# Talking-heads attention and two gated layers: another f64 conversion, and the last hand-over put into the plan

## The chip, the cores and the metric

The kernel runs on one core of a Trainium2 chip. The metric is the time of one execution on the device in microseconds (us), lower is better. The engines named here are PE (TensorE: matrix products; PEld is its weight load), DVE (VectorE: elementwise and reductions), ACT (ScalarE: activation functions and copies), POOL (GpSimd, which here only issues transfers) and SP (SyncE, which also issues transfers). A transfer that an engine's queue issues is written as SPq, ACTq or POOLq.

## What is computed

Attention in which the twelve heads are mixed before and after the softmax, then two layers of gated products. The weights of the two layers arrive as float64, so they have to be made float32 on the chip.

```python
scores = scale * np.matmul(q, k.transpose(0, 1, 3, 2))          # 4 batches, 12 heads, 448 x 448, 64 deep
scores = np.einsum('bhij,hg->bgij', scores, w_pre)
attn = exp(scores - max) / (sum + 1e-9)
attn = np.einsum('bhij,hg->bgij', attn, w_post)
x = np.matmul(attn, v)                                           # as 1792 rows of 768
x = ((x @ w1) * (x @ w2)) @ w3 @ w_out                           # 768 -> 1024 -> 768
out = np.maximum(np.maximum(x @ m1, x @ m2), x @ m3) @ m_out     # 768 wide
```

## The kernel before

**Attention** goes through 92 steps, 23 of 20 query rows for each of the four batches. Scores are computed by `unit` (PE line 345), evicted from PSUM by ACT or DVE (lines 360 and 362), stored in DRAM (`sdram`) and read back in another layout (`x`) by `regroup`. A step mixes heads (408), takes maxima and exponentials (412, 415), multiplies by the second mixing (446) and copies out (275). Every six steps `attend` multiplies by v (480). For batches 1 to 3 its result goes through the tile `xs` into DRAM (`xdram`).

**The dense work.** Before anything else the product of w3 and w_out is formed once (`fuse_parts`, line 606, result `w34`). Then batch 0 goes through the layers while batches 1 and 2 are in attention, and batch 1 while batch 3 is (`dense_parts`, line 687). Each product of float32 quality is three passes of a faster format, so every operand is split: ACT copies it to the high part (`hi`), DVE subtracts to get the low part (`lo`). A weight slab of 128 x 768 sits in one of three slab tiles (`whi`, `wlo`); `prepare` loads the slab two jobs ahead. Each of the last layer's six slabs ("o") takes 18 matmuls. Batches 2 and 3 come last and together (`last_two`), by a scheme of seven products instead of eight (`seven`, matmuls of line 219), on operands that are sums and differences of their rows: named t1, t2, t3, t4 and 22, three chunks (k = 0, 1, 2) of 128 x 448 each, and 11 and 21, which are rows of batch 2.

**Conversion of the weights** (`convert`, lines 504 to 531). A tile of float64 words is loaded by POOL's queue into `wraw` (three buffers; for w_out the tile `early`, in six places). Of each word, word(1) is its upper half and word(0) its lower. Then one ACT operation (522) and four of DVE (523, 525, 527, 529) build the float32 bits in `wc` (for w_out in the tile `v`). There are 40 tiles of 768 columns, 16 of 512 (w3) and 16 of 384 (w_out). After that ACT and DVE split it (655 and 656, 536 and 538, 571 and 572). The buffer is free for the next load when the last DVE operation has read it.

**What sets the order.** Up to the end of attention every instruction is an entry of `plan`, with an engine or a choice of two, an assumed duration, a due time and what it reads and writes. `Plan.order` runs through these with its own model and writes each engine's instructions down in the order found; each engine then executes its list strictly in order. So an instruction that waits holds up all behind it on its engine. What follows the plan is written by hand: `rest_of_one` multiplies batch 1 by the six "o" slabs (loads 236, splits 237 and 238, matmuls 219, evictions 1086, stores by ACT's queue 1087), and `attention_operands` is woven in between, one piece for every pair of chunks multiplied: it loads t3, 22, t1 and t4 from `xdram` by ACT's queue (764) and calls `layer_operands`, which subtracts (791) and splits (749, 750). These tiles lie in a pool `last` that is opened when the pool `pa` of the attention has been closed, so their loads wait until the last users of `pa` are done. The last of those are the two stores of `xs` into `xdram` after the last `attend`.

Of the kernel before, what the change touches and what calls it, by code (L numbers as in the profile page):

```python
# [8 lines left out]
F32 = mybir.dt.float32  # L9
# [28 lines left out]
F64_MIN = 2.0 ** -15  # L38
F64_MAX = 122880.0

# [135 lines left out]
def attention_talking_heads_moe_kernel(  # L176
# [327 lines left out]
    def convert(key, src, w, after=(), early=None):  # L504
# [10 lines left out]

        def word(x):
            return to().bitcast(U32).rearrange("p (x two) -> p x two", two=2)[:, :, x]
# [119 lines left out]
    KEPT = len(DENSE) - KX  # L637
# [114 lines left out]
    def attention_operands(X):  # L752

        last = tail["pool"]
        rows = tail["x"] = {}
        for n, name in enumerate(("11", "21")):
            rows[name] = [[t[:, n * QK + k] for k in range(QK)] for t in X[APART]]
        f = {}
        for name, b, x in (("t3", 1, 0), ("22", 1, 1), ("t1", 0, 0), ("t4", 0, 1), ("t2", 0, 2)):
            hi, lo = (last.tile([P, QK, S], F32R, tag=name + y, name=name) for y in ("hi", "lo"))  # L760
            rows[name] = [[t[:, k] for k in range(QK)] for t in (hi, lo)]
            if x < 2:
                f[name] = lo.bitcast(F32)
                nc.scalar.dma_start(f[name], xdram[APART + b][x * QK:(x + 1) * QK].rearrange("x p i -> p x i"))
        yield
        for k in range(QK):
            v = {"11": f["t1"][:, k], "21": f["t4"][:, k], "12": f["t3"][:, k], "22": f["22"][:, k]}
            yield from layer_operands(rows, k, v, ("11", "21"))
# [72 lines left out]
    def weight_groups(name, i, n):  # L841

        yield split_group(kept[name, i], 2 * HW)
# [249 lines left out]
    for _ in rest_of_one():  # L1093
        step()
# [49 lines left out]
```

## Time and profile before

| what | before |
|---|---|
| time, median of 3 runs (lowest to highest) | 1164.87 us (1164.27 to 1166.12) |
| the profiled execution's own time | 1165.8 us |
| its span from first to last instruction | 1164.0 us |
| PE busy | 1104.3 us (95%) |
| DVE busy | 839.9 us (72%) |
| ACT busy | 542.8 us (47%) |
| chain that ended last, by engine | PE 81%, DMA 10%, DVE 4%, ACT 2% |
| granted PE clock, mean of the span | 0.975 of full speed |

Busy times come from one profiled execution. "Busy" of PE counts overlapping matmuls of modelled length, so the step from the start of one matmul to the start of the next is the better measure of PE's pace. A row of a timeline gives start and length in us, engine, line, operation, output and inputs, shape, and in brackets how long the engine had been idle and what ended that. A trailing x2 means two in a row in one row.

### The profile page before, as it was taken

To read this page: it belongs to the slowest core of one execution; us is meant where nothing else is said; L and a number is where in the kernel's file an instruction comes from. 1 tells how busy PE (TensorE), PEld (TensorE's weight loads), DVE (VectorE), ACT (ScalarE), POOL (GpSimd) and SP (SyncE) were. 2 spreads that over 40 slices of the span, in tenths; PEclk is the share of its full clock that TensorE was granted. 3 is DMA by queue.
4 is the path that set the end of the run, shared out by engine and by line. 5 is a ranking of instruction groups with operands and counts; after the bars stand their busy time and mean duration, and the time that the engine had idled before them with its cause. 6 is when DMAs were issued, how large, how long until landed. Compare 5 with 4: busy or idle time off the path is not lost.

```text
span 1164.0 us, 29307 instructions
## 1 busy us (share of the span) xinstructions
PE 1104.3 (95%) x12348; PEld 892.4 (77%) x12348; DVE 839.9 (72%) x1452; ACT 542.8 (47%) x1034; POOL 74.5 (6%) x141
## 2 busy tenths in 40 slices
PE   3689999999999999999999999998899999999998
PEld 0256768777878778787876778877788899988987
DVE  3788777788965888987666678772877754587874
ACT  3455554565565656555444454442533334332331
POOL 3010000000000000000111101110000000000000
PEclk8579999999999999999999999999899999999999
DMA  8889879869995797989999898965433321233343
GB/s 253 244 278 307 264 224 325 257 221 323 300 321 155 254 308 255 346 280 303 303 287 305 286 308 281 309 200 194 153 99 109 107 85 50 75 109 109 102 117 122
DMA packets 118318, 259.82 MB, mean 223 GB/s; under 512 B 23446, under 2 KB 72106, under 8 KB 118186
## 3 DMA queue, kind: packets, MB, share of 16 engines
q1 hardware_dynamic: 97994, 172.75, 46.7%
q0 software_dynamic: 15584, 77.62, 20.4%
q10 hardware_dynamic: 4608, 7.57, 1.8%
q8 instruction: 97, 1.59, 0.6%
q14 instruction: 35, 0.29, 0.1%
HBM read 175.13 MB, written 82.77 MB: 222 GB/s over the span
## 4 chain that ended last, share of the span: by engine, by line
PE 81%; DMA 10%; DVE 4%; ACT 2%; issue 1%; POOL 0%; SPq 0%; ACTq 0%; DVEq 0%; POOLq 0%
PE w L687 26%; PE w L219 9%; PE p L446 7%; PE p L219 6%; PE p L480 6%; PE m L219 6%; PE s L219 6%; PE m L408 6%; PE s L345 5%; PE w L606 5%; DMA sdram<-s 2%; DMA wraw<-in_wa 1%; DMA sdram<-a 1%; DMA early<-in_w_out 1%; DMA t<-xdram 1%
## 5 line engine op out<-in xcount | busy, mean ns | idle before, releaser
L446 PEld LDWEIGHTS p<-kwr,e 60*64 60x64 f32 x5760 | 103.6, 137 | 43.3 <-issue 29.1
L415 ACT ACTIVATE e<-m,nmax 128x448 f32<-128x448 f32 (+1 forms) x184 | 115.3, 635 | 39.0 <-DVE nmax L412 38.9
L412 DVE TENSOR_REDUCE nmax<-m 128x2 f32<-128x896 f32 (+1 forms) x92 | 100.1, 1088 | 43.2 <-PE m L408 42.6
L446 PE MATMUL p<-kwr,e 60*64 60x60 f32 x5760 | 106.1, 221 | 3.7 <-DVE kwr L422 1.7
L275 ACT COPY a<-p 128x480 f32<-128x480 f32 (+1 forms) x109 | 59.9, 574 | 96.9 <-PE p L446 91.6
L408 PE MATMUL m<-x,kp 60*64 60x448 f32 x720 | 91.9, 564 | 7.7 <-ACT e L415 4.9
L345 PE MATMUL s<-kall,q 64*64 64x448 f32 x640 | 82.7, 587 | 15.5 <-DMA q<-in_qT 10.2
L687 PE MATMUL w<-yhi,whi 128*128 128x448 f32 x216 | 82.8, 383 | 0.1
L687 PE MATMUL w<-yhi,wlo 128*128 128x448 f32 x216 | 79.2, 367 | 0.8 <-DVE wlo L663 0.8
L687 PE MATMUL w<-ylo,whi 128*128 128x448 f32 x216 | 79.0, 366 | 0.0
L480 PEld LDWEIGHTS p<-a,v 128*64 128x64 f32 x1536 | 73.7, 137 | 6.8 <-issue 3.9
L480 PE MATMUL p<-a,v 128*64 128x120 f32 (+1 forms) x1536 | 78.0, 261 | 0.0
L687 PE MATMUL w<-xhi,whi 128*128 128x448 f32 x192 | 74.5, 388 | 0.7 <-DVE t L275 0.5
L687 PE MATMUL w<-xhi,wlo 128*128 128x448 f32 x192 | 70.5, 367 | 1.8 <-DVE wlo L663 1.8
L687 PE MATMUL w<-xlo,whi 128*128 128x448 f32 x192 | 70.2, 365 | 0.0
L749 ACT CAST whi<-wlo 128x768 fp32r<-128x768 f32 x40 | 33.4, 835 | 76.6 <-DMA wlo<-sums_m 20.8
L360 ACT ACTIVATE s<-s 128x896 f32<-128x896 f32 x52 | 47.7, 917 | 38.3 <-PE s L345 28.7
L275 DVE COPY a<-p 128x480 f32<-128x480 f32 x71 | 46.0, 654 | 23.2 <-ACT a L275 18.2
L219 PE MATMUL p<-t,vhi 128*128 128x448 f32 x204 | 61.7, 373 | 0.0
L663 DVE TENSOR_TENSOR wlo<-wlo,whi 128x768 fp32r<-128x768 f32 (+1 forms) x46 | 47.0, 1022 | 19.8 <-ACT whi L662 19.6
L522 ACT ACTIVATE wc<-wraw 128x768 f32<-128x768 f32 (+1 forms) x56 | 47.4, 848 | 28.7 <-DMA wraw<-in_w3T 8.5
L749 ACT CAST vhi<-vlo 128x768 fp32r<-128x768 f32 (+1 forms) x40 | 26.9, 674 | 68.9 <-DMA vlo<-sums_m 22.1
(226 smaller groups left out, 2610.2 us busy)
## 6 DMA issues: line engine op xcount, KB each, us to landing
x<-sdram SPq DMA_DIRECT2D x176, 210.0 KB
sdram<-s SPq DMA_DIRECT2D x66, 448.0 KB
wraw<-in_wm POOLq DMA_DIRECT2D x18, 768.0 KB, 6.6
wlo<-kept_m SPq DMA_DIRECT2D x27, 384.0 KB
wlo<-kept_w SPq DMA_DIRECT2D x18, 512.0 KB
wraw<-in_w3T POOLq DMA_DIRECT2D x16, 512.0 KB, 7.3
kept_m<-wc SPq DMA_DIRECT2D x18, 384.0 KB
wc<-kept_m POOLq DMA_DIRECT2D x18, 384.0 KB, 7.1
```

Of the source, the lines that this page charges most:

```text
L219: nc.tensor.matmul(out, w, r, start=(k == 0), stop=(k == 3 * n_k - 1))
L275: (nc.scalar.copy if e == "ACT" else ENG[e].tensor_copy)(out, src)
L345: nc.tensor.matmul(pt[HB * c:HB * c + HB, o, :S], qs[slot][sl, pr, i:i + HB], kall[sl, pr], start=True, stop=True)
L360: nc.scalar.activation(out, pt[:, :, :S], AF.Copy, scale=D ** -0.5)
L408: nc.tensor.matmul(pm[HB * c:HB * c + HB, u, :S], kp[sl], x[sl, c], start=True, stop=True)
L412: plan("DVE", 1.1, key + 0.01, lambda _: nc.vector.tensor_reduce(out=nmax[:r], in_=pm[:r, :, :S], axis=AX.X, op=ALU.max, negate=True), m_b ...
L415: plan("ACT", 0.85, key + 0.02, lambda _, u=u: nc.scalar.activation(e_[:r, u], pm[:r, u, :S], AF.Exp, bias=nmax[:r, u:u + 1], scale=1.0, a ...
L446: nc.tensor.matmul(pt[HB * side:HB * side + HB, c, t, :, u * GB:u * GB + m], e_[sl, u, j:j + HB], kwr[sl, u, :, :m], start=True, stop=True,)
L480: nc.tensor.matmul(pt[o * D:(o + 1) * D, x, pr % 3, :], vt[:, jc, h * D:(h + 1) * D], a[:, jc, h, :], start=(jc == 0), stop=(jc == JC - 1),)
L606: nc.tensor.matmul(pw[b][:, :FW], w, r, start=(k == 0 and i == 0), stop=(k == KH - 1 and i == 2))
L687: nc.tensor.matmul(pw[w][:, :S], u, r, start=(k == 0 and i == 0), stop=(k == nk - 1 and i == 2))
L749: nc.scalar.copy(hi, t)
```

## The change

Two things change, apart from the names in code that follows from them.

`convert` builds the float32 bits in another way. DVE clamps word(1), read as float32 with its sign, to plus or minus 122880 (one operation, from the strided `wraw` to `wc`). ACT then applies a parametric relu that scales by 2^-112 and gives negative values a slope of -2^32, so that the sign ends up as a bit of the exponent. A second ACT operation, which needs nothing of these, copies word(0) in place as an integer scaled by 7.49 * 2^-32, which leaves its top three bits. One DVE operation shifts `wc` left by three and ors these bits in. ACT has two operations for one, DVE two for four. ACT still loads its table of functions once, as before.

The hand-over at the end of the plan is now in the plan. Batch 1's "o" jobs are the last jobs of `dense_parts` (so `rest_of_one` is gone, and their stores go by SP's queue). `attention_operands` is replaced by `tail_parts`, a fifth stream of the plan: closing `pa` and opening `last`, the four loads by SP's queue, the differences and splits, and the first two weight groups of `last_two`, each with a due time. The lists `weight_groups` and `whole_slab` give functions instead of tiles, so that the first two groups can be skipped where they were made already.

```diff
-        plan("ACT", 0.88 * f, key, lambda _: nc.scalar.activation(t, word(1).bitcast(F32), AF.Abs), raw, wc)
         plan("DVE", 0.14 + 0.43 * f, key, lambda _: nc.vector.tensor_scalar(
-            t, t, F64_MIN, F64_MAX, op0=ALU.max, op1=ALU.min), (), wc)
-        plan("DVE", 0.14 + 0.43 * f, key, lambda _: nc.vector.tensor_scalar(
-            ti, ti, 5, 2, op0=ALU.logical_shift_left, op1=ALU.logical_shift_right), (), wc)
+            t, word(1).bitcast(F32), -F64_MAX, F64_MAX, op0=ALU.max, op1=ALU.min), raw, wc)
+        plan("ACT", 0.08 + 0.76 * f, key, lambda _: nc.scalar.activation(
+            t, t, AF.Prelu, scale=EXPONENT, alpha=SIGN), (), wc)
+        plan("ACT", 0.08 + 0.84 * f, key, lambda _: nc.scalar.activation(word(0), word(0), AF.Copy, scale=TOP), raw, low)
         plan("DVE", 0.16 + 0.8 * f, key, lambda _: nc.vector.scalar_tensor_tensor(
-            ti, word(0), 29, ti, op0=ALU.logical_shift_right, op1=ALU.bitwise_or), raw, wc)
-        plan("DVE", 0.16 + 0.8 * f, key, lambda _: nc.vector.scalar_tensor_tensor(
-            ti, word(1), 0xC0000000, ti, op0=ALU.bitwise_and, op1=ALU.bitwise_or), raw, wc)
+            ti, ti, 3, word(0), op0=ALU.logical_shift_left, op1=ALU.bitwise_or), raw + low, wc)
...
+    def tail_parts(pool_users, at_):
...
+        def move(_):
+            stages.close()
+            last = tail["pool"] = ctx.enter_context(tc.tile_pool(name="last", bufs=1))
...
+        n = plan("SP", 0.0, at_(0), move, (), [("moved",)])
+        plan.ops[n][3].update(pool_users)
...
+        for name, b, x in names[:4]:
+            dma("SP", at_(1), lambda name=name: tiles[name][1].bitcast(F32),
+                xdram[APART + b][x * QK:(x + 1) * QK].rearrange("x p i -> p x i"), 688e3,
+                [("moved",)] + [("xd", APART + b, c, x) for c in range(NCH)], [("l", name, k) for k in range(QK)])
...
+        def difference(k, x, y, reads):
+            n = turn("r", 3)
+            plan("DVE", 0.63, at_(3 + k), lambda _: nc.vector.tensor_sub(spares[n], x(), y()), reads, [("r", n)])
...
+        def split(k, name, value):
+            src, reads = value
+            plan("ACT", 0.57, at_(3 + k), lambda _: nc.scalar.copy(tiles[name][0][:, k], src()), reads, [("h", name, k)])
+            plan("DVE", 0.64, at_(3 + k), lambda _: nc.vector.tensor_sub(
...
-        yield from dense_parts(1, DENSE[:KEPT], second_at)
+
+    def second_stream():
+
+        yield TURN + 0.01
+        yield from dense_parts(1, DENSE, second_at)
+
+    def tail_stream():
+
+        yield second_at(126.5)
+        yield from tail_parts(pool_users, lambda x: LAST + 2.2 + 0.8 * x)
...
-    behind.append(attention_operands(X))
-    for _ in rest_of_one():
-        step()
-    flush()
+    for g in tail["made"]:
+        next(tail["groups"])
+        made.append(g)
     for _ in last_two():
         step()
```

SP's list at the hand-over, from the last slabs of the layer before to the first weight groups. `kept_o` are the "o" slabs, `xdram_82` is batch 3 and `xdram_81` batch 2, `t` and `22` the operands. Before:

```order
L270 DMA wlo<-kept_m_5_118 128x768
L236 DMA wlo<-kept_o_119 128x768
L236 DMA wlo<-kept_o_120 128x768
L270 DMA xdram_82<-xs 128x3x88 x2
L236 DMA wlo<-kept_o_121 128x768
L837 DMA vlo<-sums_a_125 128x768
L236 DMA wlo<-kept_o_122 128x768
L837 DMA vlo<-kept_a_93 128x384
```

After:

```order
L272 DMA wlo<-kept_m_5_118 128x768
L272 DMA wlo<-kept_o_119 128x768
L272 DMA xdram_82<-xs 128x3x88 x2
L272 DMA wlo<-kept_o_120 128x768
L272 DMA t_8795<-xdram_82 128x3x448
L272 DMA 22_8797<-xdram_82 128x3x448
L272 DMA t_8799<-xdram_81 128x3x448
L272 DMA wlo<-kept_o_121 128x768
L272 DMA t_8801<-xdram_81 128x3x448
L272 DMA wlo<-kept_o_122 128x768
```

The four operand loads moved from ACT's queue into SP's, the second "o" slab now stands behind the stores of `xs`, and the third and fourth stand among the operand loads.

DVE's list at the same place: maxima of the layer before (717, now 718), low parts of "o" slabs (238, now 664), differences (791, now 788) and their low parts (750, now 794). Before:

```order
L238 TENSOR_TENSOR wlo<-wlo,whi 128x768 x2
L717 TENSOR_TENSOR t<-w,t 128x448
L704 TENSOR_TENSOR hlo<-t,hhi 128x448
L791 TENSOR_TENSOR t_8909<-t_8890,t_8896 128x448
L791 TENSOR_TENSOR t_8917<-22_8893,t_8909 128x448
L238 TENSOR_TENSOR wlo<-wlo,whi 128x768
```

After:

```order
L664 TENSOR_TENSOR wlo<-wlo,whi 128x768
L718 TENSOR_TENSOR t<-w,t 128x448
L705 TENSOR_TENSOR hlo<-t,hhi 128x448
L277 COPY t<-w 128x448
L788 TENSOR_TENSOR r<-t_8795,t_8799 128x448
L788 TENSOR_TENSOR r<-22_8797,r 128x448
L794 TENSOR_TENSOR t_8799<-r,t_8798 128x448
L788 TENSOR_TENSOR r<-22_8797,t_8795 128x448
L664 TENSOR_TENSOR wlo<-wlo,whi 128x768
```

The third slab's low part stands behind a difference of t3 and t1 in both lists; before it two more operations stand there now, and the eviction of the first "o" product has come to DVE.

DVE's list where the tiles of w_out are converted (`early` is the float64 tile, `v` the result, `hlo` its low part). Before:

```order
L525 TENSOR_SCALAR v<-v 128x384
L572 TENSOR_TENSOR hlo<-v,hhi 128x384
L527 SCALAR_TENSOR_TENSOR v<-early,v 128x384
L525 TENSOR_SCALAR v<-v 128x384
L529 SCALAR_TENSOR_TENSOR v<-early,v 128x384
L527 SCALAR_TENSOR_TENSOR v<-early,v 128x384
L523 TENSOR_SCALAR v<-v 128x384
```

After:

```order
L526 TENSOR_SCALAR v<-early 128x384 x2
L574 TENSOR_TENSOR hlo<-v,hhi 128x384
L531 SCALAR_TENSOR_TENSOR v<-v,early 128x384
L526 TENSOR_SCALAR v<-early 128x384
L531 SCALAR_TENSOR_TENSOR v<-v,early 128x384
L574 TENSOR_TENSOR hlo<-v,hhi 128x384 x2
L531 SCALAR_TENSOR_TENSOR v<-v,early 128x384
L526 TENSOR_SCALAR v<-early 128x384
```

Five DVE operations for a tile have become three, and ACT's relu (528) lies between the first and the second of them. In the whole program 17 evictions of scores moved from ACT to DVE (360, 362: 52 and 26 before, 35 and 43 after).

## Rows read from the trace of the kernel before

**Rows 1.** Windows by stage: busy us of each engine, granted clock, DMA share, GB/s.

```profile
45.00:90.00 45.00, 36.10 (x218) 23.25 (x218) 38.07 (x96) 25.50 (x50) 7.93 (x14) 0.75 0.83 267
...
225.00:570.00 345.00, 343.20 (x4902) 271.90 (x4898) 273.90 (x454) 198.31 (x383) 22.25 (x41) 1.00 0.86 281
...
797.00:837.00 40.00, 31.12 (x217) 28.20 (x216) 22.05 (x35) 16.85 (x31) 0.00 (x0) 0.87 0.57 189
```

**Rows 2.** Timeline of PE across the hand-over: start us, length us, operation.

```profile
801.67 0.47 PE L687 MATMUL w<-yhi,whi 128*128 128x448 f32 x1
...
802.99 0.36 PE L219 MATMUL w<-hhi,whi 128*128 128x448 f32 x1
...
810.08 0.37 PE L219 MATMUL w<-hhi,wlo 128*128 128x448 f32 x1
819.33 0.74 PE L219 MATMUL w<-hhi,whi 128*128 128x448 f32 x1 [8.88 <-ACT o L1086]
...
825.04 0.37 PE L219 MATMUL w<-hhi,whi 128*128 128x448 f32 x1
...
836.59 0.37 PE L219 MATMUL m<-xhi,whi 128*128 128x448 f32 x1
```

**Rows 3.** Timeline of ACT across the hand-over.

```profile
801.78 0.66 ACT L275 COPY xs<-p 128x264 f32<-128x264 f32 x2 [1.06 <-PE p L480]
...
804.78 0.41 ACTq L764 DMA_DIRECT2D t<-xdram  x1
...
807.50 0.84 ACT L237 CAST whi<-wlo 128x768 fp32r<-128x768 f32 x1 [3.08 <-PE w L219]
```

**Rows 4.** Timeline of DVE across the hand-over.

```profile
817.62 0.62 DVE L791 TENSOR_TENSOR t<-t,t 128x448 f32<-128x448 f32 x1 [12.55 <-DMA t<-xdram]
...
818.82 0.95 DVE L238 TENSOR_TENSOR wlo<-wlo,whi 128x768 fp32r<-128x768 f32 x1
```

**Rows 5.** Timeline of SP's queue across the hand-over.

```profile
802.19 0.90 SPq L270 DMA_DIRECT2D xdram<-xs  x2
803.21 0.45 SPq L236 DMA_DIRECT2D wlo<-kept_o  x1
```

**Rows 6.** Window of the wait at the hand-over, columns as in rows 1.

```profile
810.00:815.00 5.00, 0.45 (x3) 0.07 (x1) 0.00 (x0) 0.00 (x0) 0.00 (x0) 0.97 1.05 394
```

**Rows 7.** Groups by line and shape: count, busy us, mean ns, idle before.

```profile
L522 ACT ACTIVATE wc<-wraw 128x768 f32<-128x768 f32 x40 | 36.7, 918 | 20.2 <-DVE wlo L656 6.0 <-DMA wraw<-in_wa 5.4 <-DMA kept_b<-wc 3.0
L655 ACT CAST whi<-wc 128x768 fp32r<-128x768 f32 x40 | 33.4, 836 | 12.8 <-DVE wc L529 7.1 <-PE w L687 5.6
L523 DVE TENSOR_SCALAR wc<-wc 128x768 f32<-128x768 f32 x40 | 22.2, 555 | 13.8 <-ACT wc L522 13.5
L527 DVE SCALAR_TENSOR_TENSOR wc<-wraw,wc 128x768 uint32<-128x768 uint32 x40 | 38.2, 954 | 0.6
```

**Rows 8.** Windows while the tiles of w_out are converted, columns as in rows 1.

```profile
50.00:55.00 5.00, 3.14 (x10) 2.31 (x11) 5.00 (x14) 3.03 (x7) 1.61 (x3) 0.84 0.73 215
...
65.00:70.00 5.00, 4.09 (x23) 2.56 (x23) 3.67 (x10) 3.95 (x8) 0.68 (x2) 1.00 0.99 386
...
80.00:85.00 5.00, 3.96 (x18) 2.33 (x15) 4.55 (x10) 3.22 (x5) 0.00 (x0) 0.50 0.33 129
```

**Rows 9.** Timeline of DVE while the tiles of w_out are converted.

```profile
55.17 0.55 DVE L529 SCALAR_TENSOR_TENSOR v<-early,v 128x384 uint32<-128x384 uint32 x1
...
57.12 0.55 DVE L529 SCALAR_TENSOR_TENSOR v<-early,v 128x384 uint32<-128x384 uint32 x1
```

**Rows 10.** Timeline of ACT in the same stretch.

```profile
52.55 0.99 ACT L522 ACTIVATE v<-early 128x384 f32<-128x384 f32 x2
...
76.64 0.56 ACT L522 ACTIVATE v<-early 128x384 f32<-128x384 f32 x1 [1.03 <-DMA early<-in_w_out]
```

**Rows 11.** PE's waits from 90 to 797 us: total us, times, longest.

```profile
PE w L687 <- DVE wlo L663: 2.6, 4, 1.1
PE m L408 <- ACT e L415: 2.3, 2, 1.2
```

More of the change, by code (lines that the diff above doesn't have):

```diff
@@ L37 @@
 RB = 6
-F64_MIN = 2.0 ** -15
 F64_MAX = 122880.0
+EXPONENT = 2.0 ** -112
+SIGN = -2.0 ** 32
+TOP = 7.49 * 2.0 ** -32
 def blocks_of(p):
@@ L514, in convert @@
             raw = [(f"X{'hl'[z]}", x)]
+        low = [("low", raw[0])]
         def word(x):
@@ L636, in attention_talking_heads_moe_kernel @@
     DENSE += [(KX, (f"m{x}", m)) for m in range(KX) for x in range(3)] + [(KX, ("o", m)) for m in range(KX)]
-    KEPT = len(DENSE) - KX
     def dense_parts(b, jobs, at_):
@@ L841, in weight_groups @@
     def weight_groups(name, i, n):
-        yield split_group(kept[name, i], 2 * HW)
-        yield split_group(sums[name, i][:, :2 * HW], 2 * HW)
-        yield split_group(sums[name, i][:, 2 * HW:], 2 * HW)
-        yield split_group(kept[name, i + n][:, HW:], HW)
+        yield lambda: split_group(kept[name, i], 2 * HW)
+        yield lambda: split_group(sums[name, i][:, :2 * HW], 2 * HW)
+        yield lambda: split_group(sums[name, i][:, 2 * HW:], 2 * HW)
+        yield lambda: split_group(kept[name, i + n][:, HW:], HW)
     def whole_slab(m):
-        yield [t.rearrange("p k f -> p (k f)") for t in slab(KH, ("w34", m))]
+        yield lambda: [t.rearrange("p k f -> p (k f)") for t in slab(KH, ("w34", m))]
     def all_groups():
@@ L870, in look_ahead @@
                 break
-            made.append(g)
+            made.append(g())
     def group():
@@ L917, in last_two @@
     def last_two():
-        x = tail["x"]
+        x = {name: [[t[:, k] for k in range(QK)] for t in pair] for name, pair in tail["tiles"].items()}
+        for n, name in enumerate(("11", "21")):
+            x[name] = [[t[:, n * QK + k] for k in range(QK)] for t in rows("X")]
         last = tail["pool"]
@@ L1060, in summing @@
         yield from sum_parts(sums_at)
-    streams = [attention_parts(), dense_stream(), summing()]
-    heads = [(-20.0 + x, x) for x in range(3)]
+    streams = [attention_parts(), dense_stream(), summing(), second_stream(), tail_stream()]
+    heads = [(-20.0 + x, x) for x in range(5)]
     heapq.heapify(heads)
+    pool_users = []
     while heads:
         _, x = heapq.heappop(heads)
+        n = len(plan.ops)
         key = next(streams[x], None)
+        if x < 3:
+            pool_users += range(n, len(plan.ops))
         if key is not None:
@@ L1072, in attention_talking_heads_moe_kernel @@
         plan.emit()
-    X = {APART: rows("X")}
-    def rest_of_one():
-        ready = [slab(KX, ("o", m)) for m in range(2)]
-        for m in range(KX):
-            hi, lo = ready.pop(0)
-            pt = bank()[:, :S]
-            zh, zl = rows("H")
-            yield from products(pt, [(hi[:, k], lo[:, k], zh[:, k], zl[:, k]) for k in range(KX)], KX)
-            if m + 2 < KX:
-                ready.append(slab(KX, ("o", m + 2)))
-            o = scratch("o")
-            nc.scalar.copy(o, pt)
-            nc.scalar.dma_start(outT[m * P:(m + 1) * P, S:2 * S], o)
-    stages.close()
-    tail["pool"] = ctx.enter_context(tc.tile_pool(name="last", bufs=1))
     tail["groups"] = all_groups()
-    behind.append(attention_operands(X))
-    for _ in rest_of_one():
-        step()
-    flush()
+    for g in tail["made"]:
+        next(tail["groups"])
+        made.append(g)
     for _ in last_two():
```

49 lines of the change are left out of this document (34 added, 15 removed).

## The prediction

> **What bounds the kernel now.** I read the windows by stage first, then PE's timeline where a window is not full, then the lists of the engines that PE waited for. From 225 to 570 us PE is busy 343.20 of 345 us at full clock, while DVE is busy 273.90 and ACT 198.31 [rows 1]: there PE sets the time, and a cheaper conversion is worth only what it takes away of PE's own waits. Over the whole stretch from 90 to 797 us these are 8.6 us in eight groups, the two largest 2.6 and 2.3 [rows 11]. So the time is to be looked for in two stages. From 45 to 90 us PE is busy 36.10 of 45 at a mean clock of 0.75, and from 797 to 837 us 31.12 of 40 at 0.87 [rows 1].
>
> At the hand-over PE steps from 802.99 to 810.08 in 35 matmuls, 0.203 us each, stops for 8.88, and then takes 5.71 us for the 15 matmuls up to 825.04, where 15 at 0.203 would be 3.04 [rows 2]. The granted clock in the 15 is the lower of the two levels (0.5 of full); it fell during the idle time. From the end of attention's last product (801.67) to the first matmul of the seven products (836.59) are 34.92 us for 6 + 108 matmuls, which at 0.203 need 23.1. **The hand-over costs 11.8 us.** Its cause stands on DVE: the low part of the third "o" slab (818.82) waits in line behind a difference that waits 12.55 us for the operand loads [rows 4], issued by ACT at 804.78 [rows 3], after the stores of `xs` at 802.19 [rows 5]. The core's transfers run at 394 GB/s meanwhile [rows 6].
>
> From 45 to 80 us the sixteen tiles of w_out are converted. DVE is busy all 5.00 us of a window while the transfers move 215 GB/s; fifteen us later ACT and DVE wait for tiles that arrive, at 386 GB/s [rows 8, 10]. A tile takes DVE 1.95 us (57.12 less 55.17) [rows 9]. PE's products need these tiles in order.
>
> **The hand-over, part by part.** I count from A, the end of the last attention product (801.67 before). The order puts 24 matmuls of the layer before and of the first slab behind it (six before), then the rest of the 108.
> - The `xs` stores are issued at about A+0.5, the second "o" slab right behind them, at A+1.5 (the third slab's place before: 803.21 [rows 5]); before it went ahead of them. A load issued there was in place by A+5.8, when ACT's copy of it began [rows 3]. Copy 0.84, low part 0.95: A+7.6. PE gets to it after 36 matmuls, at A+7.3, and has to wait for the maximum on DVE that frees the PSUM bank, queued behind that low part: A+8.0. **A wait of 0.7.**
> - The operand loads follow at A+3.1 (804.78 before). t3, 22 and t1 are 2.06 MB, 5.3 us at 394 GB/s [rows 6]; with 1.8 ahead of the first byte and some 1.5 behind the last (estimates: the wait before was 12.8 from the issue at 804.78 to 817.62, with 3.5 to 4.1 MB moving, 9 to 10 us at that rate) they are there at A+11.5 to A+12. Here they have the queue nearly to themselves, since the third slab's load must wait for PE to free its tile at A+7.3 and stands behind them. The fourth load, t4, is held up by this one and lands at about A+14.5.
> - PE finishes the first slab at A+11.7 and the second at A+12.9 (12 + 6 + 6 matmuls after A+8.0). ACT then evicts the second (0.5), copies t1 (0.57) and only then the third slab (0.84): A+14.8. DVE does four operations of 0.55 to 0.62 and that slab's low part: A+16.1. PE waits 1.9, does two matmuls, and waits 0.9 more. **Together 2.8.** After that the lists are ahead of PE: the fourth slab's low part ends at A+19.3 and PE arrives there at A+19.35.
> - The last k of the operands is ready at about A+35: DVE has some 24 us of operations from A+11.7 on, and PE needs the last t3 at about A+37. That holds by two us.
>
> So 3.5 us of waits stay of 11.8, in pieces of at most 2 us, and the clock stays up: **-8.3 us.** Bounds: if the loads are there sooner all goes (-11.8); if they are there as late as before, or the clock falls in the waits as well, 4 to 5 more stay (-3.5). What hides the differences and splits now is the 22 us of "o" products, and the cover is thin: DVE is full from A+12 to A+35.
>
> **The conversion, part by part.** A tile of 768 columns costs ACT 0.918 and DVE 2 x 0.555 + 2 x 0.954 = 3.02 before [rows 7]. After, DVE does one operation like 527 (0.954) and a clamp. The clamp reads every second word of `wraw`, which 523 does not: 0.555 if that costs nothing, 0.954 if it runs as slowly as 527, which does read so; I take 0.555, the row of the same operation. ACT does the relu, in rows between 0.836 (a copy of dense words) and 0.918 (strided), and the integer copy, 0.918, with a strided output that no row shows; up to 1.0. DVE falls by 1.1 to 1.5 us a tile, ACT rises by 0.84 to 1.0. In tiles of 768 there are 58.7 (40 + 16 x 2/3 + 16 x 1/2), so DVE loses 65 to 88 us of work and ACT gains 49 to 59, less 17 evictions moved to DVE. From 225 to 570 neither fills up: ACT would come to about 220 of 345 and DVE to about 235 [rows 1]. So there it lies beside PE.
>
> The Trainium skill ("VectorE: DVE Perf Modes", What auto-detection actually checks) says that an operation of one source, with source and destination in SBUF and their outermost dimensions even, is done two elements at a time, and asks no dense words of it for 32-bit data. By that the clamp costs 0.555; at 0.954 ACT and DVE would be level below and the stage would gain some 2 us less. No row before shows a strided clamp.
>
> From 45 to 80 us it is on the path. A tile of 384 takes DVE there 1.95; without two operations of 0.27 and 0.47 step it is 1.2 to 1.4. ACT's three operations step by 0.42 to 0.45 (two in 0.99 less the overlap [rows 10]): 1.3 a tile, 21 us for sixteen. Added to this are about five evictions of scores at 0.9 and an exponential pair that now stands here: 28 us from about 46, so the last tile at 74, where DVE took until 78 before. ACT takes DVE's place as the limit, and the transfers are a second limit close to it (386 GB/s near the end [rows 8]). **-3 us, between 0 and -6.** Up to 4 us more could come if the clock, which is at its lower level from 80 to 85 [rows 8], stayed up.
>
> The waits from 90 to 797 us come out anew, since the order of all engines is another; with DVE lighter by a quarter those behind it should shrink, those behind ACT grow. **-1, between -5 and +5.** The first 45 us keep their chain of stores and reads: no change, 1 us either way. The tail after 837 us keeps its code: none.
>
> **The sum.** -8.3 - 3 - 1 = -12.3. The profiled execution took 1165.8, 0.9 above the median: 1153.5 there, 1152.6 as a median, forecast **1153 us**.
>
> **Rivals.**
> - *The wait is only moved.* PE stops at the third slab long enough for the clock to fall again, as it did in the 8.88 us. For it: the slab's load, the differences and the slab's low part still stand in line behind t1, and from 80 to 85 us the clock is at its lower level though PE is busy 3.96 of 5 [rows 8], so a stop of 9 us is not needed for that. Against: the stops are shorter than the one before by two thirds. 4 us less gain: 1157; with nothing in the first stage 1160.
> - *The first stage gives more.* The tiles arrive as fast as ACT takes them, the lower clock of 80 to 85 us is gone, and the waits of rows 11 fall by half: 7 more, 1146.
> - *Slower: the convoy.* Each conversion now crosses from DVE to ACT and back to DVE, and both execute in order, so an exponential can stand behind a relu that waits for a clamp. If such a stop cost PE 1.2 us (the longest behind an exponential [rows 11]) in each of the 40 conversions of 768 columns, it would be 48 us; from about ten on it eats the gain of the hand-over, and twenty give +24 - 8 - 3, 1178. Against: DVE and ACT are idle for a fifth and two fifths of that stage [rows 1].
> - *Nothing moves*: the first operand loads land no sooner, the conversion stays hidden: 1163 to 1166.
>
> **How the numbers follow.** Forecast (1148 to 1157) 0.52; the wait moved (1156 to 1161) 0.18; the first stage gives more (1141 to 1148) 0.16; convoy 0.08; nothing moves 0.06. The range 1143 to 1161 leaves out the convoy, most of the last and the end of the third. A difference of 0.2% (2.3 us) is about what a measurement of this kernel can tell from none. Faster by more than that is 0.52 + 0.18 + 0.16 and a little of the last, 0.87; within it 0.06; slower 0.07.
>
> **What would show it.** Right: PE's timeline has no stop above 3 us between the last `attend` and the seven products, and the granted clock there is 1; from A to the first product of the seven are 30 to 31 us for 132 matmuls; the clamp of 768 columns has a mean near 555; sixteen tiles of w_out end near 74; ACT busy rises by 30 to 45 us and DVE falls by 40 to 70. Wrong: a clamp near 950, a stop with a fallen clock at the third slab, or PE stops behind exponentials and splits between 225 and 570 us, which would be the convoy.

## The result: 1145.2 us, 19.7 less than before

The changed kernel takes 1145.2 us (median of 4 runs, 1144.16 to 1146.06), the kernel before 1164.86. The ratio is 0.9829, 95% interval 0.9812 to 0.9846. The profiled execution took 1146.06 us with a span of 1144.3. The time lies in the range of the prediction, 7.8 us under the forecast of 1153, at the rival "the first stage gives more" (1146).

These are the windows by stage of the changed kernel, columns as in [rows 1]; the last row is the hand-over, which now begins earlier:

```profile
45.00:90.00 45.00, 37.56 (x442) 26.81 (x434) 36.95 (x84) 36.66 (x84) 7.47 (x14) 0.87 0.89 288
90.00:225.00 135.00, 133.00 (x2272) 102.27 (x2272) 86.79 (x164) 80.69 (x168) 8.43 (x16) 1.00 0.91 288
225.00:570.00 345.00, 342.54 (x4898) 271.17 (x4901) 253.58 (x426) 203.76 (x385) 22.55 (x42) 1.00 0.86 280
...
787.00:822.00 35.00, 31.59 (x145) 27.98 (x144) 25.91 (x41) 18.17 (x31) 0.00 (x0) 0.95 0.70 230
```

From 45 to 90 us PE executes 442 matmuls where it executed 218 [rows 1], at a clock of 0.87 for 0.75. From 225 to 570 next to nothing has changed for PE, though DVE has 20 us less to do. The groups of the conversion, columns as in [rows 7]:

```profile
L531 DVE SCALAR_TENSOR_TENSOR wc<-wc,wraw 128x768 uint32<-128x768 uint32 x40 | 37.9, 955 | 11.5 <-ACT wc L528 11.3
L530 ACT ACTIVATE wraw<-wraw 128x768 uint32<-128x768 uint32 x40 | 36.7, 917 | 4.5 <-DMA wraw<-in_wm 4.4
L528 ACT ACTIVATE wc<-wc 128x768 f32<-128x768 f32 x40 | 33.3, 846 | 16.6 <-DVE wc L526 16.6
L526 DVE TENSOR_SCALAR wc<-wraw 128x768 f32<-128x768 f32 x40 | 21.7, 553 | 0.1
```

The strided clamp takes 553 ns, like the dense one before (555 [rows 7]); the rule of the Trainium skill that the prediction weighed ("VectorE: DVE Perf Modes", What auto-detection actually checks) agrees with this trace. Relu and integer copy, 846 and 917 ns, lie near the lower end of what was given for each (836 to 918, and 918 up to 1000).

**Where the time came from.** Sums of idle time don't show it well, since a stop of PE also costs the start of the next matmul, and a low clock is no idle time. So each matmul gets a standard step, from the stretches at full clock of both kernels: 0.203 us in the layers, 0.174 for w3 times w_out (all of them ahead of 217 us), 0.095 for scores, 0.108 and 0.020 for the two mixings, 0.053 for the product with v. The **lost time** at a matmul is its start less the standard steps of all matmuls ahead of it. The whole work is 1069.2 us by these steps. It is read where 35, 730 and 760 us of work are done, which in the kernel before is at 92, 800 and 841.5 us. Each row of such a table is of one profiled execution.

| lost time, us | to 92 | 92 to 800 | hand-over | rest | sum |
|---|---|---|---|---|---|
| before | 57.0 | 13.0 | 11.4 | 9.3 | 90.7 |
| changed | 49.8 | 5.7 | 5.9 | 9.6 | 71.0 |
| forecast for the difference | -3 | -1 | -8.3 | 0 | -12.3 |
| measured difference | -7.2 | -7.3 | -5.5 | +0.3 | -19.7 |

### The profile page after: what moved, and what is told of

It is laid out like the page before. It is cut to its first block, busy times and chain, and to the rows that moved or that the text cites. A ratio compares the mean times of both kernels' runs of the same rounds, so it can differ in the third digit from the quotient of the medians.

```text
span 1144.3 us, 29231 instructions
## 1 busy us (share of the span) xinstructions
PE 1095.7 (96%) x12348; PEld 889.3 (78%) x12348; DVE 787.0 (69%) x1347; ACT 562.9 (49%) x1067; POOL 74.0 (6%) x141
## 4 chain that ended last, share of the span: by engine, by line
PE 89%; DMA 4%; DVE 3%; ACT 3%; issue 1%; POOL 0%; SPq 0%; DVEq 0%; ACTq 0%; POOLq 0%
PE w L688 32%; PE w L221 8%; PE p L448 8%; PE p L482 6%; PE p L221 6%; PE m L410 6%; PE m L221 6%; PE s L221 6%; PE w L608 5%; PE s L347 5%; DMA sdram<-a 1%; DMA x<-sdram 1%; DMA vlo<-sums_o 1%; DMA wraw<-in_w3T 1%; DMA wlo<-kept_m 0%
## 5 line engine op out<-in xcount | busy, mean ns | idle before, releaser
L277 ACT COPY a<-p 128x480 f32<-128x480 f32 (+1 forms) x101 | 55.5, 575 | 83.1 <-PE p L448 80.6
L347 PE MATMUL s<-kall,q 64*64 64x448 f32 x640 | 80.3, 568 | 11.8 <-DMA q<-in_qT 8.7
L277 DVE COPY a<-p 128x480 f32<-128x480 f32 (+1 forms) x79 | 50.8, 652 | 28.8 <-ACT a L277 19.2
L688 PE MATMUL w<-hhi,whi 128*128 128x448 f32 x168 | 64.7, 385 | 2.6 <-ACT whi L663 1.8
L664 DVE TENSOR_TENSOR wlo<-wlo,whi 128x768 fp32r<-128x768 f32 (+1 forms) x52 | 52.8, 1015 | 18.7 <-ACT whi L663 18.4
L531 DVE SCALAR_TENSOR_TENSOR wc<-wc,wraw 128x768 uint32<-128x768 uint32 (+1 forms) x56 | 49.0, 879 | 20.8 <-ACT wc L528 17.6
L688 PE MATMUL w<-hhi,wlo 128*128 128x448 f32 x168 | 62.3, 371 | 0.9 <-DVE wlo L664 0.8
```

The source lines that it names most:

```text
L277: (nc.scalar.copy if e == "ACT" else ENG[e].tensor_copy)(out, src)
L347: nc.tensor.matmul(pt[HB * c:HB * c + HB, o, :S], qs[slot][sl, pr, i:i + HB], kall[sl, pr], start=True, stop=True)
L664: plan("DVE", 0.16 + 0.8 * f, key - 0.9, lambda _: nc.vector.tensor_sub(lo, t, hi.bitcast(F32)), h, l)
L688: nc.tensor.matmul(pw[w][:, :S], u, r, start=(k == 0 and i == 0), stop=(k == nk - 1 and i == 2))
```

## The experiments

### One part alone

`tail_only` has `convert` of before and all else of the change; `convert_only` has the kernel before with the new `convert`. Up to the hand-over the lists of PE, ACT and DVE are, row for row, those of the kernel before in the first (but for one pair of PE's that is swapped in the trace), and those of the changed kernel in the second, so the two take the change apart.

```diff
 # tail_only, in the changed kernel
-        plan("DVE", 0.14 + 0.43 * f, key, lambda _: nc.vector.tensor_scalar(
-            t, word(1).bitcast(F32), -F64_MAX, F64_MAX, op0=ALU.max, op1=ALU.min), raw, wc)
...
+        plan("ACT", 0.88 * f, key, lambda _: nc.scalar.activation(t, word(1).bitcast(F32), AF.Abs), raw, wc)
...
```

> The old conversion (one operation on ACT, four on DVE) with the new hand-over in the plan. Up to the hand-over the lists of PE, ACT and DVE are those of the kernel before. Theory (the two parts add up: hand-over some 6 us, the rest of the 19.7 from the conversion): 1157 to 1161 us, the stretch from 45 to 90 us with the lower clock near 80 as before, PE's waits from 90 to 797 us as before, and at the hand-over stops of 1 to 2 us instead of one of 8.88. Rival (the hand-over gives what was forecast and more, 8 to 12 us): 1153 to 1157.

> The new conversion with the old hand-over. Up to the hand-over the lists are those of the changed kernel. Theory: the first 800 us are 13 to 14 us shorter and the hand-over costs 11 to 12 us as before: 1150 to 1153 us. Rival (the two need each other: with the old hand-over the earlier end of attention only lengthens the wait for the operand loads): 1156 to 1161, and PE's stop at the hand-over longer than 10 us.

| | time, us | ratio to before, 95% interval | to 92 | 92 to 800 | hand-over | rest |
|---|---|---|---|---|---|---|
| `tail_only` | 1156.6 | 0.9949 (0.9931 to 0.9966) | 53.0 | 13.4 | 6.1 | 9.3 |
| `convert_only` | 1150.5 | 0.9887 (0.9860 to 0.9915) | 48.7 | 6.9 | 8.4 | 12.6 |

The two ratios multiplied are 0.984, and the change gave 0.983: the parts add up, some 6 us from the hand-over and 13 from the rest. The hand-over of `tail_only` is not as smooth as was expected of it: its longest stop, at the fourth slab, is 3.06 us, and the clock falls behind it. In `convert_only` PE stops 6.57 us at the hand-over instead of 8.88, with 134 matmuls between the last attention product and the seven for 114. It loses 3 us more in the rest, where PE waits 1.2 us more for DVE and the clock is at its lower level for 3.4 us once. `tail_only` also shows how far one list spreads from run to run: with the lists of the kernel before it lost 53.0 us to 92, and the kernel before 57.0. Over half of that arises behind 78 us and goes with the clock: the row of `tail_only` from 80 to 85 us (columns as in [rows 1]) has full clock, where the kernel before had the lower level [rows 8]. Behind 92 us the two agree within half a us, 13.4 and 13.0.

```profile
80.00:85.00 5.00, 4.63 (x34) 3.35 (x30) 4.97 (x10) 3.43 (x8) 0.00 (x0) 1.00 0.31 99
```

### Which tiles

`wout_old` is the changed kernel with only the 16 tiles of w_out converted the old way, `wout_new` has only these converted the new way, `w3_old` has only the 16 tiles of w3 (512 columns) converted the old way.

```diff
 # wout_old; wout_new has "is None" here, w3_old has "early is None and w < PW"
+        if early is not None:
+            plan("ACT", 0.88 * f, key, lambda _: nc.scalar.activation(t, word(1).bitcast(F32), AF.Abs), raw, wc)
...
+        else:
+            plan("DVE", 0.14 + 0.43 * f, key, lambda _: nc.vector.tensor_scalar(
...
```

> The changed kernel, but the sixteen tiles of w_out are converted the old way; the other 56 and the hand-over are new. Theory A (the 7 us between 70 and 90 us come from those sixteen tiles being ready earlier): they are lost again, the lower clock near 80 us is back, 1150 to 1154 us. Theory B (they come from the order of the scores' evictions around, or from w3, which is also new): 1143 to 1148. Theory C (any new order of the lists shifts the waits by several us either way): the stages do not add up, PE's waits from 90 to 797 us differ from both kernels by more than 3 us though the conversions there are those of the changed kernel.

> The counterpart: only the sixteen tiles of w_out are converted the new way, the other 56 the old way; new hand-over. Theory A: 7 us from 70 to 90 us are kept and some 6 us of waits from 90 to 797 us are as in the kernel before: 1150 to 1154 us. Theory B: the first stage stays as before, 1157 to 1161. Theory C: as for the run beside it, waits from 90 to 797 us differ by more than 3 us from the kernel before though the conversions there are its own.

> The changed kernel, but the 16 tiles of w3 (512 columns) are converted the old way; w_out and the 40 tiles of 768 columns are new. Reading of the four runs before: w_out converted the new way gains 8 to 12 us before 92 us, w3 converted the new way costs 3 to 6 there because ACT is full while both are converted, the 40 tiles gain 6 to 8 us of PE's waits from 90 to 797. Theory: these add up, 1136 to 1141 us, ACT no longer full from 55 to 70 us. Rival (the stage from 45 to 90 us comes out by the order that the plan happens to find, w3 costs nothing): 1143 to 1148.

| | time, us | ratio to before, 95% interval | to 92 | 92 to 800 | hand-over | rest |
|---|---|---|---|---|---|---|
| `wout_old` | 1155.4 | 0.9944 (0.9923 to 0.9966) | 57.9 | 7.3 | 4.7 | 9.2 |
| `wout_new` | 1149.5 | 0.9879 (0.9849 to 0.9909) | 43.8 | 15.6 | 7.0 | 10.0 |
| `w3_old` | 1144.8 | 0.9840 (0.9813 to 0.9867) | 43.2 | 11.3 | 6.4 | 9.0 |

In the first stage the kind of tile decides, as theory A had it. With w_out old it loses 53.0 to 57.9 us, with w_out new 43.2 to 49.8. The time of `wout_old` is 1.4 us above what theory A gave, that of `wout_new` half a us below. Theory C's sign did not come, since the waits from 92 to 800 are 1.6 us from the changed kernel's in the one and 2.6 from the kernel before in the other; the runs on the order, below, bear it out all the same. The last tile of w_out is done by DVE at 83.5 us before and at 78.4 after (start and length of its last DVE operation, one row of each kernel); in `wout_old` it is done at 87.7, in `wout_new` at 73.2 and in `w3_old` at 72.5, and the lost time to 92 us follows in that order:

```profile
82.94 0.55 DVE L529 SCALAR_TENSOR_TENSOR v<-early,v 128x384 uint32<-128x384 uint32 x1
```

```profile
77.86 0.55 DVE L531 SCALAR_TENSOR_TENSOR v<-v,early 128x384 uint32<-128x384 uint32 x1
```

From 80 to 85 us, where the kernel before had 18 matmuls at the lower level of the clock [rows 8], the changed kernel's row is:

```profile
80.00:85.00 5.00, 5.00 (x100) 3.56 (x96) 4.47 (x9) 3.93 (x9) 0.53 (x1) 1.00 0.99 268
```

Of the w3 tiles, which are old in `wout_new` and `w3_old`, the first stage is better by about 6 us when they are old. The reason that was expected, ACT full while both kinds are converted, does not hold: between 45 and 75 us only one w3 tile is converted in the changed kernel and none in `w3_old`, and ACT is busy 26.4 of these 30 us in the one and 26.9 in the other (two windows of it, columns as in [rows 1], first the changed kernel, then `w3_old`):

```profile
60.00:65.00 5.00, 2.96 (x17) 1.52 (x16) 4.49 (x11) 5.00 (x12) 1.39 (x3) 1.00 0.96 329
65.00:70.00 5.00, 3.98 (x16) 3.23 (x20) 4.56 (x13) 5.00 (x12) 1.62 (x4) 0.71 0.99 299
```

```profile
60.00:65.00 5.00, 3.85 (x26) 2.98 (x25) 5.00 (x12) 5.00 (x13) 2.15 (x4) 1.00 1.04 325
65.00:70.00 5.00, 5.00 (x95) 3.86 (x88) 4.93 (x14) 4.18 (x11) 0.00 (x0) 1.00 0.99 368
```

What the changed kernel has there is a place in line. The bits of its one w3 tile are done by DVE at 63.46, and the copy to the high part begins at 64.37, with operations for w_out between them on ACT's list; PE waits for both parts (timeline of ACT, of DVE, then of PE, changed kernel), and its clock is 0.71 in that window:

```profile
62.11 0.62 ACT L528 ACTIVATE wc<-wc 128x512 f32<-128x512 f32 x1
62.65 0.51 ACT L528 ACTIVATE v<-v 128x384 f32<-128x384 f32 x1
63.06 0.99 ACT L530 ACTIVATE early<-early 128x384 uint32<-128x384 uint32 x2
63.96 0.51 ACT L528 ACTIVATE v<-v 128x384 f32<-128x384 f32 x1
64.37 0.60 ACT L538 CAST whi<-wc 128x512 fp32r<-128x512 f32 x1
```

```profile
62.77 0.69 DVE L531 SCALAR_TENSOR_TENSOR wc<-wc,wraw 128x512 uint32<-128x512 uint32 x1
```

```profile
65.02 0.44 PE L608 MATMUL w<-hhi,whi 128*128 128x384 f32 x1 [1.49 <-ACT whi L538]
66.63 0.44 PE L608 MATMUL w<-hhi,wlo 128*128 128x384 f32 x1 [0.99 <-DVE wlo L540]
```

In `w3_old` neither stop is there. It is the fifth w3 tile, and the copy of its high part comes at another place there, ahead of the tiles of w_out:

```profile
39.46 0.61 ACT L550 CAST whi<-wc 128x512 fp32r<-128x512 f32 x1
```

The traces of all runs in this document agree: with w3 old this copy begins between 39.5 and 40.5 us in all seven kernels, with w3 new between 63.3 and 67.8 in all seven. So with the new conversion the plan leaves this tile until w_out is under way. The stretch with the two stops (from 17 to 20 us of work) makes some 3.7 of the 6.6 us between the changed kernel and `w3_old`. Some 2 us more are lost ahead of 42 us; why is open. `w3_old` as a whole is no faster than the changed kernel: what it gained to 92 us it lost in waits from 92 to 800 (11.3 for 5.7), so its time falls where the rival had it and not the theory. That the waits of this stretch take so much back led to the next runs.

### Are the waits from 92 to 800 us DVE's load?

With the 40 tiles of 768 columns old, this stretch had cost 13.0, 13.4 and 15.6 us; with them new 5.7, 6.9 and 7.3, but 11.3 in `w3_old`, which does not fit. `dve_load` puts three more clamps into each of the 40, which change nothing in the result but bring DVE's part of these conversions back to the load of before.

```diff
+        for _ in range(3 if early is None and w == PW else 0):
+            plan("DVE", 0.14 + 0.43 * f, key, lambda _: nc.vector.tensor_scalar(
+                t, t, -F64_MAX, F64_MAX, op0=ALU.max, op1=ALU.min), (), wc)
         plan("ACT", 0.08 + 0.76 * f, key, lambda _: nc.scalar.activation(
```

> The changed kernel with three more clamps of the same tile in each of the 40 conversions of 768 columns (they change nothing in the result), so that DVE has 3.17 us a tile where it had 3.02 before and 1.51 after, while ACT's work stays that of the changed kernel. Theory (PE's lost time from 92 to 797 us, 13 us with the old conversion and 6 to 7 with the new one, follows DVE's load): it comes back to 11 to 15 us, 1149 to 1154 us. Rival (it follows the number of operations that wait on each other or ACT's part): it stays at 5 to 9 us, 1143 to 1148.

It took 1145.1 us, ratio 0.9844 (0.9818 to 0.9871), and lost 7.7 us in the stretch, where the rival had it. From 225 to 570 us DVE was busier than before the change and PE just as full (window of `dve_load`, columns as in [rows 1], which has 273.90 for DVE):

```profile
225.00:570.00 345.00, 342.47 (x4831) 269.80 (x4830) 280.24 (x493) 216.64 (x407) 25.24 (x41) 1.00 0.85 279
```

So 67 us of DVE work (120 operations of 0.555) cost nothing that can be measured in the time. But it is no test of the load alone. The plan answered by giving 30 evictions from DVE to ACT, so that DVE's busy time over the whole span rose by 36 us (787.0 to 823.0, for 839.9 before), and from 163 us on the lists have another order. It shows that from 225 to 570 us such a load lies beside PE, as the prediction had it; what makes the waits needed other runs.

### The order alone

The plan assumes 0.12 us for the hop from one engine to the next. With 0.11 or 0.13 it writes down the same work in another order on every engine; with that, 3 to 23 evictions change between ACT and DVE. `order_a` is the changed kernel with 0.13, `after_hop11` with 0.11; `before_hop13` and `before_hop11` are the kernel before.

```diff
-HOP = 0.12
+HOP = 0.13
```

> The changed kernel with one assumed duration of the plan changed: the hop between engines 0.13 for 0.12 us. The same instructions, in another order on every engine from the first stage on. Theory (the stages follow the work, not the luck of the order): lost time from 92 to 797 us 5 to 8 us, 1142 to 1149 us. Rival (luck of the order): over 3 us away from the changed kernel, and that in the lost time of a stage whose work is the same.

> The kernel before with the plan's assumed hop between engines at 0.13 for 0.12 us: the same instructions in another order on every engine. In the 13 us that PE lost from 92 to 797 us before (6 to 7 after), 5 to 8 fall between 563 and 797 us, where no tile is converted any more. Theory (they are the order's, not the conversion's): the loss from 92 to 797 us becomes 6 to 10 us with the old conversion too, and the time 1155 to 1161 us, with the first stage as before. Rival (they belong to the old conversion): 12 to 16 us again, 1161 to 1167 us.

> The same with a hop of 0.11 us, a second order of the old work. Theory: 6 to 11 us lost from 92 to 797 us, 1154 to 1162 us. Rival: 12 to 16 us, 1161 to 1167.

> The changed kernel with a hop of 0.11 us in the plan: a third order of the changed work, beside the changed kernel and order_a. It shows how far the time of the same instructions spreads by their order: 1141 to 1150 us expected, with 48 to 50 us lost up to the 92nd us and 4 to 9 from there to the hand-over.

| | time, us | ratio to before, 95% interval | to 92 | 92 to 800 | hand-over | rest |
|---|---|---|---|---|---|---|
| before, 0.12 | 1164.9 | 1 | 57.0 | 13.0 | 11.4 | 9.3 |
| `before_hop11` | 1159.3 | 0.9969 (0.9953 to 0.9984) | 55.2 | 11.5 | 6.8 | 9.8 |
| `before_hop13` | 1154.4 | 0.9920 (0.9900 to 0.9940) | 52.4 | 7.9 | 5.5 | 10.1 |
| changed, 0.12 | 1145.2 | 0.9829 (0.9812 to 0.9846) | 49.8 | 5.7 | 5.9 | 9.6 |
| `order_a`, 0.13 | 1146.9 | 0.9852 (0.9821 to 0.9883) | 48.6 | 8.4 | 1.1 | 10.2 |
| `after_hop11` | 1150.8 | 0.9891 (0.9875 to 0.9907) | 49.5 | 10.3 | 6.0 | 9.6 |

The times came out near what the theories gave (`before_hop13` 0.6 and `after_hop11` 0.8 us outside), the stages less so: `order_a` has 4.8 us less at the hand-over than the changed kernel, `after_hop11` 10.3 in the waits for the 4 to 9 expected, and `before_hop11`, with 11.5, lies between theory and rival.

This is the main finding. **The same work spreads over 0.8% (9 us, before) and 0.6% (7 us, changed) by the order that the plan finds.** The kernel before had the slowest of its three orders, the changed one the fastest of its three, though `order_a` can't be told from it. The mean ratios are 0.9963 and 0.9857, so over three orders each the change is worth about 1.06%, 12 us, not 19.7; three orders that spread so far leave this uncertain by some 3 us either way (an estimate from their spread). By stage the 12 us are 5.6 to 92 us, 2.7 in the waits and 3.6 at the hand-over. The stages are of one execution each: those of `order_a` and `before_hop13` are 3.5 us under their medians, so that their rows read low. Where the lists are the same (before and `tail_only`, changed and `convert_only`), the waits from 92 to 800 agree within 1.2 us.

The first stage is the work's: 52 to 57 us with the old conversion, 48.6 to 49.8 with the new one. The waits from 92 to 800 are in large part the order's: 7.9 to 13.0 with the old work and 5.7 to 10.3 with the new. They have to be taken apart at 563 us of the kernel before, since no tile is converted behind it (the last one was done at 522). Behind it the kernel before lost 7.8 us of its 13.0, `wout_new` 7.5, the two other orders of the kernel before 2.9 and 3.2, and the kernels with the 40 tiles new 3.4 to 6.6: here the order decides. Ahead of it, over the same work, the four orders with the 40 tiles old (before, its two others, `wout_new`) lost 4.9 to 8.2, the seven with them new (changed, its two others, `wout_old`, `w3_old`, `dve_load`, `w3_old_hop13`) 0.8 to 4.8. So some 3 us of the waits, by the means, do seem to go with the conversion of these tiles. Whether through DVE's load or through the longer chain of operations that wait on each other was not separated: `dve_load`, with 4.2 there, fits both.

The rows of ACT of the kernel before show a loss of the order's kind (start, length, operation):

```profile
606.81 0.38 ACT L275 COPY xs<-p 128x264 f32<-128x264 f32 x1 [3.83 <-PE p L480]
607.09 0.84 ACT L662 CAST whi<-wlo 128x768 fp32r<-128x768 f32 x1
607.82 0.38 ACT L275 COPY xs<-p 128x264 f32<-128x264 f32 x1
608.09 0.85 ACT L662 CAST whi<-wlo 128x768 fp32r<-128x768 f32 x1
```

Two copies of slabs stand in line behind evictions that wait 3.83 us for the product with v. PE waits for the low part of the first of them at 608.97, 0.33 us; such waits are 2.6 us in four stops [rows 11]. In `before_hop13` the waits of PE for this line from 560 to 797 us have shrunk to one:

```profile
PE w L687 <- DVE wlo L663: 0.2, 1, 0.2
```

The hand-over too is partly the order's: old code in another order loses 5.5 and 6.8 us there for 11.4, about as little as the changed kernel with its 5.9, and the changed kernel in another order 1.1.

### The third slab at the hand-over

In the changed kernel ACT's copy of the third "o" slab stood behind the eviction of the second product and the copy of t1. `slab_first` orders it ahead of both, by two conditions for the plan; nothing ahead of the hand-over changes.

```diff
-                plan("ACT", 0.92 * f, key - 1.0, lambda _: nc.scalar.copy(hi, t), l, h)
+                marks[b, name] = plan("ACT", 0.92 * f, key - 1.0, lambda _: nc.scalar.copy(hi, t), l, h)
...
-                plan({"ACT": 0.55, "DVE": 0.64}, 0, key, ...
+                z = plan({"ACT": 0.55, "DVE": 0.64}, 0, key, ...
+                plan.ops[z][3].update({marks[1, ("o", 2)]} if (b, name, m) == (1, "o", 1) else ())
...
+            plan.ops[z][3].update({marks[1, ("o", 2)]} if (k, name) == (0, "t1") else ())
```

> The changed kernel with two more conditions in the plan (none on the chip): the eviction of the second 'o' product and the first copy of t1 on ACT come behind the copy of the third slab, which had landed at 796.7 while ACT stood idle from 795.3 to 797.5 in line behind the eviction. Everything up to the hand-over is unchanged. Theory (the stop at the third slab is the order on ACT and DVE, and the fallen clock follows from it): the stops of 1.82 and 0.79 us shrink to under 1.2 together, the clock stays up, 2 to 3.5 us less than the changed kernel: 1141.5 to 1143.5 us. Rival (the operands become the last thing): the wait moves to the first of the seven products, 1144 to 1147.

It took 1144.7 us (1140.0 to 1145.95), ratio 0.9827 (0.9788 to 0.9865), which can't be told from the changed kernel: the gain that the theory gave is not shown in the time. Its profile shows a smaller effect: 3.8 us lost at the hand-over for 5.9, stops of 1.33 and 0.32 us for 1.82 and 0.79, where under 1.2 together were expected, and full clock behind them. First PE's timeline and ACT's, then the window from 800 to 805 us of `slab_first`:

```profile
798.98 0.47 PE L688 MATMUL w<-hhi,whi 128*128 128x448 f32 x1 [1.33 <-ACT whi L663]
...
799.97 0.47 PE L688 MATMUL w<-hhi,wlo 128*128 128x448 f32 x1 [0.32 <-DVE wlo L664]
```

```profile
798.10 0.83 ACT L663 CAST whi<-wlo 128x768 fp32r<-128x768 f32 x1 [1.39 <-DMA wlo<-kept_o]
```

```profile
800.00:805.00 5.00, 5.00 (x24) 4.57 (x25) 4.88 (x9) 3.45 (x6) 0.00 (x0) 1.00 0.88 297
```

ACT now waits for the load of the slab itself. It is issued at 791.68, when PE frees the slab's tile, and is there 6.4 us later, when the copy begins; the load of t1 is issued at 788.21 ahead of it and that of t4 at 792.07 behind it. The slab's load is the next thing late. The operands were not.

### A faster version

> A candidate that may beat both kernels: w3 converted the old way, the other tiles the new way, and the plan's hop at 0.13 us. w3_old lost 43 us up to the 92nd us where the changed kernel lost 50, and gave it back in waits from 92 to 797 us (11.3 for 5.7). Theory (the first is the work's, the second the order's): 43 to 45 us lost at first, 6 to 9 then, 1134 to 1141 us. Rival (fewer operations on ACT at first mean more waits later, in any order): 1143 to 1147.

`w3_old_hop13` takes 1138.7 us (1137.6 to 1139.2), ratio 0.9789 (0.9774 to 0.9803). By the ratios, each to the kernel before as timed beside it, that is 4.7 us less than the changed kernel (6.5 by the times). It lost 44.3 us to 92, 7.3 from there to 800, 1.5 at the hand-over and 11.1 in the rest. The first two are as the theory had them: the gain of the first stage came again in another order, and with it the early place of the fifth w3 tile (40.3 us), so it goes with the kind of conversion; the waits from 92 to 800 of `w3_old` were in part the order's. That the hand-over costs 1.5 was not aimed at; `order_a` and `dve_load`, with the same order of PE's matmuls there, lose 1.1 and 1.5.

## Why the prediction was right, and where it was off

**The bound** was read rightly: the stages from 225 to 570 us are PE's, and the 27 us that DVE has more there in `dve_load` than in the changed kernel do not show in the time.

**The total** fits the mean over three orders each, 12 us, but in part by luck. By terms that mean is -5.6, -2.7 and -3.6 for the -3, -1 and -8.3 of the forecast: too little in the first stage and in the waits, too much at the hand-over. For the two kernels as they stand the hand-over gave less than forecast too, and the other two terms lie outside their ranges.

**The hand-over, -8.3 forecast, -5.5 measured.** From the first matmul behind the last attention product (783.85, as 801.67 before) to the first of the seven (816.54) are 32.69 us for 132 matmuls; 30 to 31 were forecast. The three stops were forecast as 0.7, 1.9 and 0.9; PE's timeline of the changed kernel shows 0.81, 1.82 and 0.79:

```profile
783.85 0.47 PE L688 MATMUL w<-yhi,whi 128*128 128x448 f32 x1
...
792.22 0.44 PE L688 MATMUL w<-hhi,whi 128*128 128x448 f32 x1 [0.81 <-DVE t L718]
...
799.23 0.47 PE L688 MATMUL w<-hhi,whi 128*128 128x448 f32 x1 [1.82 <-ACT whi L663]
799.54 0.36 PE L688 MATMUL w<-hlo,whi 128*128 128x448 f32 x1
800.69 0.51 PE L688 MATMUL w<-hhi,wlo 128*128 128x448 f32 x1 [0.79 <-DVE wlo L664]
801.00 0.57 PE L688 MATMUL w<-hhi,whi 128*128 128x448 f32 x1
...
803.99 0.56 PE L688 MATMUL w<-hhi,wlo 128*128 128x448 f32 x1
804.36 0.39 PE L688 MATMUL w<-hhi,whi 128*128 128x448 f32 x1
...
816.54 0.36 PE L221 MATMUL m<-xhi,vhi 128*128 128x448 f32 x1
```

What the sum left out is the clock. From 801.00 to 804.36 nine matmuls take 0.373 us each, at the lower level of the clock, 1.5 us more than at 0.203. And each stop costs some 0.27 beyond its idle time: 799.23 is 2.18 behind the matmul ahead of it, 0.16 more than a step and the idle time, and the next step is 0.31. So the rival "the wait is only moved" came true in its mechanism, the clock falling again at the third slab, which the prediction named as a sign of being wrong; the price was 1.5 us instead of 4. The tail's order of steps (loads at A+3, the slab's load behind t1, ACT's eviction ahead of its copy) was as forecast.

One reading of the stop before was incomplete. PE's row [rows 2] names ACT's eviction (1086) as what ended the 8.88 us, not the low part of the third slab, which ended at 819.77. ACT's list has that eviction behind a copy (749) that waits for the same difference, so the late operand loads held up both (ACT of the kernel before):

```profile
818.28 0.56 ACT L749 CAST t<-t 128x448 fp32r<-128x448 f32 x1 [9.95 <-DVE t L791]
818.75 0.53 ACT L1086 COPY o<-w 128x448 f32<-128x448 f32 x1
```

**The first stage, -3 (0 to -6) forecast, -7.2 measured**, of which up to 4 is run-to-run spread (`tail_only`). The tiles of w_out come 5.1 us earlier; 4 were forecast, though from a wrong end: the prediction let DVE take until 78 before, and it was 83.5. The "4 us more if the clock stayed up" were set aside as a possibility; they came. This was the rival with the chance of 0.16.

**The waits from 90 to 797 us, -1 (-5 to +5) forecast, -7.3 measured.** This is the step that failed. The prediction took the 8.6 us of waits [rows 11] as typical of the old work and let them come out about the same. They were a poor draw: the same work in two other orders loses less, most clearly where nothing is converted. In idle time, the measure of the prediction, the waits fell from 8.6 to 5.2 us; the rest of the 7.3 should be what each stop costs beyond its idle time, and delays too short to be listed as waits. Its bound of 5 was too small as well; by the runs a new order can move this stretch by 5 us and the hand-over by 5 to 6. The reason given for a small gain, DVE lighter by a quarter, is not shown: from 225 to 570 us DVE became lighter by 7% (273.90 to 253.58), `dve_load` put that back and lost 7.7 us where the kernel before lost 13.0, and some 3 us that seem to go with the conversion may have another cause.

**The conversion's prices** held: clamp 553, ACT's first and second operation 846 and 917. Convoys of exponentials behind relus did not appear: the waits of PE for exponentials from 90 to 797 us, 2.3 before [rows 11], are gone from the list of the changed kernel. ACT's busy time rose by 20.1 us and DVE's fell by 52.9, where 30 to 45 and 40 to 70 were forecast; more evictions than the 17 of scores had moved from ACT to DVE (8 copies of `a` and 5 of `xs` among them). So from 225 to 570 us ACT came to 204 and DVE to 254 us, for the 220 and 235 of the prediction. Of the waits behind ACT, which were to grow, one kind came in: PE's for copies of `xs`, 2.5 us.

## What to carry to other kernels

Where a planner writes the order, time two or three orders of the old and of the new work (one assumed duration moved by a hundredth will do) before a gain of one per cent is credited to an edit: here, over three orders each, some 12 of 19.7 us were the change's and some 7 the draw's. An operation taken from an engine that isn't the bound is worth what it moves forward in the stage where that engine is full, and little elsewhere: 16 of 72 tiles gave what the conversion gave in its own stage, and the 40 of the long stretch behind it some 3 us at most. In a hand-over, look for what stands in line ahead of the next load's consumer on its engine, and expect a new last thing behind it.

## What was not expected of the hardware

The clock decides several us in places where the idle time hardly differs: the lists of the kernel before ran from 80 to 85 us once at 0.50 and once (`tail_only`) at 1.00, and the changed kernel's clock fell behind stops of 1.82 and 0.79 us, while that of `slab_first` stayed up behind 1.33 and 0.32. The length of the stops alone does not tell: behind 1.64 and 0.32 us it fell (`before_hop11`), behind 1.60 and 0.33 it stayed up (`before_hop13`). An integer copy in place on ACT that reads and writes every second word takes 917 ns for 768 columns, no more than the one that only read so before (918 [rows 7]).
